# An attention and FFN kernel: scores, values and FFN in blocks, loads issued first, and q and k transposed by DMA instead of TensorE

## The chip, the cores and the metric

The kernel runs on one core of one Trainium2 chip. The metric is the device time of one launch in microseconds (us). Besides timed launches there is one profiled execution of each kernel; its length on the core is called the span, and it is about 1.7 to 1.8 us shorter than the time of the same launch. All launches quoted here count as fast runs: no second, slower state was seen, and the granted TensorE clock, a mean over the span, was between 0.97 and 1.0 in all of them.

Engines are named as in the profile: PE is the matrix engine (TensorE), PEld its weight load, DVE is VectorE, ACT is ScalarE, POOL is GpSimd, SP is SyncE. In this kernel POOL and SP issue the DMAs. "L181" is a line of the kernel that was profiled, so line numbers differ from kernel to kernel.

## The reference, cut to what matters

Block-sparse attention over 4 batches, 8 heads, 768 positions and 64 channels, followed by a multiplicative feed-forward network.

```python
scores = scale * np.matmul(q, k.transpose(0, 1, 3, 2))       # [4, 8, 768, 768], D = 64
mask = near the diagonal | first and last block | 3 random blocks per row of 32-blocks
attn = softmax(np.where(mask, scores, -1e9))
x = np.matmul(attn, v) -> [3072, 512]
a = x @ w1                                                    # 512 x 1024
b = x @ w2
h = a * b @ w3                                                # 1024 x 1024
out = h @ w_out                                               # 1024 x 512, float32
```

The kernel folds `w3 @ w_out` into one matrix once, so that the FFN needs three matrix products per token block (`pa`, `pb`, `po`).

## The kernel before

The work is cut into 72 groups, 18 per batch. A group is (b, t, Q, kp): a batch, a third of the queries, four heads, and two of the six key chunks. For each group PE makes two tiles of scores (two heads each, four matmuls 64x128 on 256 columns); ACT takes the exponential of a tile (1.025 us), and DVE multiplies it by the mask (0.69 us). The values of a group are taken one group later, so that ACT and DVE have time. After every third group the output `o` is divided by the denominator `d`: ACT does a logarithm and an exponential, DVE a multiplication, and only then can the next values write `o` and `d`, which have one buffer each.

Everything else PE has to do is put into a queue of "fill" items, and `pop(n)` emits n of them: first the weight fold (`fold_transpose`, four PE transposes and a DVE copy; `fold_mm`, four matmuls 128x512), later the FFN (`pa`, `pb`, `po`, four matmuls 128x512 each). The order in which PE, ACT and DVE get their instructions is the order of the program.

```python
ps_s = pool("ps_s", 2, space=PSUM)    # score tiles, and also the PE transposes of q and k
ps_o = pool("ps_o", 1, space=PSUM)    # o and d
ps_f = pool("ps_f", 2, space=PSUM)    # all fill items

def transposes(b, pr):                # q and k of two heads: [token, channel] -> [channel, token]
    tp = ps_s.tile([128, 2, 1024], BF16, tag="s", name="tp")
    for x, src in ((0, qn[b, pr]), (1, kn[b, pr])):
        for c in range(C):
            for h in range(2):
                nc.tensor.transpose(tp[64 * h:64 * h + 64, x, c * 128:(c + 1) * 128],
                                    src[:, h, c, :], ident)
    t = qkt.tile([128, 2, S], BF16, tag="qkt", name="qkt")
    nc.vector.tensor_copy(t, tp[:, :, :S])
    QK[b, pr] = t

# (cut: scores, values, normalize, ffn)

for i in range(NF):                   # NF = 8: all fold transposes first ...
    fill.append(fold_transpose(i, 0))
    fill.append(fold_transpose(i, 1))
for i in range(NF):                   # ... then all fold matmuls
    fill.extend(fold_mm(i))

for s, g in enumerate(groups):
    b, t, Q, kp = g
    r = s % 18
    # (cut: transposes(0, 2) and (0, 3) at groups 5 and 7)
    if b + 1 < B:
        if r in (2, 5, 8, 11):
            load_pair(b + 1, (r - 2) // 3)
        if r in (12, 13, 15, 16):
            transposes(b + 1, (12, 13, 15, 16).index(r))
    n = 0 if s < 7 else (3 if s < 18 else 2)
    scores(b, t, Q, kp, 0)
    pop(n // 2)
    scores(b, t, Q, kp, 1)
    if prev is not None:
        values(*prev)
        finish(prev)                  # normalizes after kp == 2, and queues FFN items
    pop(n - n // 2)
    prev = g
```

The softmax here doesn't subtract the row's maximum and nothing guards it: scores larger than these inputs give would overflow.

Of the kernel before, what the change touches and what calls it, by code (L numbers as in the profile page):

```python
# [8 lines left out]

F32 = mybir.dt.float32  # L10
BF16 = mybir.dt.bfloat16
I32 = mybir.dt.int32
AF = mybir.ActivationFunctionType
ALU = mybir.AluOpType
# [4 lines left out]
def kernel(  # L19
# [16 lines left out]
    nc = tc.nc  # L36
    B, H, S, D = q.shape
    BLK = 32
    NB = S // BLK
    C = S // 128  # L40
    d_model = H * D
    d_ff = moe_w1.shape[1]
    NF = d_ff // 128
# [3 lines left out]
    def pool(name, bufs, **kw):  # L47
        return ctx.enter_context(tc.tile_pool(name=name, bufs=bufs, **kw))

    const = pool("const", 1)  # L50
    wts = pool("wts", 1)
    nat = pool("nat", 4)
    natv = pool("natv", 8)
    qkt = pool("qkt", 8)
# [24 lines left out]
    rand_sb = const.tile([NB, 6], I32, tag="rand_sb")  # L79
    nc.sync.dma_start(out=rand_sb, in_=sampled_blocks.bitcast(I32))  # L80

    def load_pair(b, pr):
        for src, dst, pl, tag in ((qv, qn, nat, "qn"), (kv, kn, nat, "kn"), (vv, vn, natv, "vn")):
            t = pl.tile([128, 2, C, D], BF16, tag=tag, name=tag)
            nc.gpsimd.dma_start(out=t, in_=src[b][:, 2 * pr:2 * pr + 2])  # L85
            dst[b, pr] = t

    w1_sb = wts.tile([128, 4, d_ff], BF16, tag="w1")
    w2_sb = wts.tile([128, 4, d_ff], BF16, tag="w2")
    w3_sb = wts.tile([128, NF, d_ff], BF16, tag="w3")  # L90
    w3t_sb = wts.tile([128, NF, d_ff], BF16, tag="w3t")
    wo_sb = wts.tile([128, NF, d_model], BF16, tag="wo")
    wf_sb = wts.tile([128, NF, d_model], BF16, tag="wf")

    def load_w12(ap, t):
        src = ap.rearrange("(Q g s d) f -> g d Q s f", Q=2, g=4, s=2)
        for g in range(4):
            for Q in range(2):
                nc.gpsimd.dma_start(out=t[32 * g:32 * g + 32, 2 * Q:2 * Q + 2, :], in_=src[g][:, Q])


    ident = const.tile([128, 128], BF16, tag="ident")
    make_identity(nc, ident)
    ones = const.tile([128, 32], BF16, tag="ones")
    nc.vector.memset(ones, 1.0)

    hot = const.tile([NB, C, 128], BF16, tag="hot")
    nc.gpsimd.memset(hot, 1.0)
    nc.gpsimd.affine_select(out=hot, in_=hot, compare_op=ALU.is_ge, fill=0.0, base=0,
                            pattern=[[1, C], [C, 128]], channel_multiplier=-BLK)  # L110
    nc.gpsimd.affine_select(out=hot, in_=hot, compare_op=ALU.is_ge, fill=0.0, base=BLK - 1,
                            pattern=[[-1, C], [-C, 128]], channel_multiplier=BLK)
    JJ = const.tile([NB, NB], F32, tag="JJ")
    nc.gpsimd.iota(JJ, pattern=[[1, NB]], base=0, channel_multiplier=0,
                   allow_small_or_imprecise_dtypes=True)
    II = const.tile([NB, NB], F32, tag="II")
    nc.gpsimd.iota(II, pattern=[[0, NB]], base=0, channel_multiplier=1,
                   allow_small_or_imprecise_dtypes=True)
    DD = const.tile([NB, NB], F32, tag="DD")
    nc.gpsimd.iota(DD, pattern=[[-1, NB]], base=0, channel_multiplier=1,  # L120
                   allow_small_or_imprecise_dtypes=True)
    load_pair(0, 0)
    load_pair(0, 1)

    A = const.tile([NB, NB], F32, tag="A")
    nc.vector.tensor_tensor(DD, DD, DD, op=ALU.mult)
    nc.vector.tensor_scalar(A, in0=DD, scalar1=1.0, scalar2=None, op0=ALU.is_le)
    for src in (II, JJ):
# [5 lines left out]
    for r in range(3):  # L134
# [3 lines left out]
                                op=ALU.is_equal)  # L138
# [21 lines left out]
    QK = {}  # L160

    def transposes(b, pr):
# [5 lines that stand above are left out]
                                        src[:, h, c, :], ident)  # L168
        t = qkt.tile([128, 2, S], BF16, tag="qkt", name="qkt")
        nc.vector.tensor_copy(t, tp[:, :, :S])  # L170
        QK[b, pr] = t

    E = {}

    def scores(b, t, Q, kp, i):
        qk = QK[b, 2 * Q + i]
        s = ps_s.tile([128, 2, 512], F32, tag="s", name="s")
        for k2 in range(2):
            kc = 2 * kp + k2
            for h in range(2):  # L180
                nc.tensor.matmul(s[:, h, k2 * QT:(k2 + 1) * QT],  # L181
                                 lhsT=qk[64 * h:64 * h + 64, 1, kc * 128:(kc + 1) * 128],
                                 rhs=qk[64 * h:64 * h + 64, 0, t * QT:(t + 1) * QT],
                                 start=True, stop=True)
        e = epool.tile([128, 2, 512], BF16, tag="e", name="e")
        nc.scalar.activation(e, s, AF.Exp, scale=1.0 / 8.0)  # L186
        nc.vector.tensor_tensor(e, e, mask[:, t, kp:kp + 1, :].to_broadcast((128, 2, 512)),  # L187
                                op=ALU.mult)
        E[b, t, Q, kp, i] = e
# [43 lines left out]
    fill = deque()  # L233

    def fold_transpose(i, jh):
        def go():
            tp = ps_f.tile([128, 4, 128], BF16, tag="f", name="w3p")
            for j in range(4):
                nc.tensor.transpose(tp[:, j, :],  # L239
                                    w3_sb[:, i, (4 * jh + j) * 128:(4 * jh + j + 1) * 128], ident)  # L240
            nc.vector.tensor_copy(w3t_sb[:, 4 * jh:4 * jh + 4, i * 128:(i + 1) * 128], tp)  # L241
        return go

    def fold_mm(i):
        box = {}

        def part(jh):
            def go():
                if jh == 0:
                    box["p"] = ps_f.tile([128, 512], F32, tag="f", name="wp")  # L250
                for j in range(4 * jh, 4 * jh + 4):
                    nc.tensor.matmul(box["p"], lhsT=w3t_sb[:, j, i * 128:(i + 1) * 128],  # L252
                                     rhs=wo_sb[:, j, :], start=j == 0, stop=j == NF - 1)
                if jh == 1:
                    nc.vector.tensor_copy(wf_sb[:, i, :], box["p"])
            return go
        return [part(0), part(1)]
# [48 lines left out]


    transposes(0, 0)
    transposes(0, 1)
    load_pair(0, 2)  # L310
    load_pair(0, 3)
    nc.gpsimd.dma_start(out=w3_sb, in_=moe_w3.rearrange("(c r) f -> r c f", r=128))
    nc.gpsimd.dma_start(out=wo_sb, in_=moe_w_out.rearrange("(c r) f -> r c f", r=128))
    load_w12(moe_w1, w1_sb)
    load_w12(moe_w2, w2_sb)
    for t in range(NT):
        build_mask(t)

# [6 lines left out]
    for i in range(NF):  # L325
        fill.append(fold_transpose(i, 0))
        fill.append(fold_transpose(i, 1))
    for i in range(NF):
        fill.extend(fold_mm(i))

    done = {}
# [3 lines left out]
    def finish(g):  # L335
        nonlocal n_ffn
        b, t, Q, kp = g
        if kp == 2:
            normalize(b, t, Q)
            done[b * NT + t] = done.get(b * NT + t, 0) + 1  # L340
            while done.get(2 * n_ffn) == 2 and done.get(2 * n_ffn + 1) == 2:
                ffn(n_ffn)
                n_ffn += 1

    def pop(n):
        for _ in range(n):
            if fill:
                fill.popleft()()

    for s, g in enumerate(groups):  # L350
        b, t, Q, kp = g
        r = s % 18
        if b == 0 and s == 5:
            transposes(0, 2)
        if b == 0 and s == 7:
            transposes(0, 3)
        if b + 1 < B:
            if r in (2, 5, 8, 11):
                load_pair(b + 1, (r - 2) // 3)
            if r in (12, 13, 15, 16):  # L360
                transposes(b + 1, (12, 13, 15, 16).index(r))
        n = 0 if s < 7 else (3 if s < 18 else 2)
        scores(b, t, Q, kp, 0)
        pop(n // 2)
        scores(b, t, Q, kp, 1)
        if prev is not None:
            values(*prev)
            finish(prev)
        pop(n - n // 2)
        prev = g  # L370
    values(*prev)
    finish(prev)
# [33 lines left out]
```

## Time and profile before

| quantity | value | where it is read |
|---|---|---|
| time, median of 3 launches | 308.6 us (307.41 to 308.62) | launch times |
| profiled span | 305.1 us | page |
| PE busy | 93% | busy table |
| chain that ended last | 85% PE | chain of waits |
| start of group 0 (first scores) | 19.17 us | timeline |
| start of group 18 (batch 1) | 80.28 us | timeline |
| start of group 71 (the last) | 264.50 us | timeline |
| a steady group | 3.36 us | timeline, group to group |

From the page of the kernel before: the busy table (busy us, share of the span, instructions), the chain that ended last by engine, the group of DVE copies that empty the transposes (operation, shapes, count, then busy us and mean ns of one, then idle time before them and what ended it), and the DMA queue that loads inputs (packets, MB, share of 16 engines).

```profile
PE 282.8 (93%) x3412; PEld 129.2 (42%) x3412; DVE 188.1 (62%) x303; ACT 194.1 (64%) x250; POOL 48.0 (16%) x78
...
q0 software_dynamic: 16416, 14.68, 31.2%
...
PE 85%; ACT 6%; DVE 3%; POOL 2%; DMA 2%; issue 1%; ACTq 0%; POOLq 0%
...
L170 DVE COPY qkt<-tp 128x1536 bf16<-128x1536 bf16 x16 | 15.3, 956 | 7.0 <-PE tp L167 6.5
```

PE bounds the kernel. Where its time goes is better read from start to start in the timeline of PE than from durations: the length of a matmul record includes a tail in which the next matmul already runs (below, the record of 140.82 lasts 1.04 us, and the next one starts 0.97 us after it). The columns of the timeline are start in us, length in us, engine and line, operation, tiles, shapes and count, and in brackets the idle time before it and what ended that. First the start of the kernel before, then one of its steady groups, between 140.50 and 143.85 us.

```profile
7.37 0.60 PE L147 MATMUL gp<-hot,Ab 24*24 24x512 bf16 x1 [7.37 <-DVE Ab L141]
...
19.17 1.03 PE L181 MATMUL s<-qkt 64*128 64x256 bf16 x8
...
59.98 1.90 PE L252 MATMUL wp<-wo_sb,w3t_sb 128*128 128x512 bf16 x8
61.82 0.39 PE L181 MATMUL s<-qkt 64*128 64x256 bf16 x4
...
66.03 0.53 PE L167 MATMUL tp<-ident,qn 128*64 128x128 bf16 x12
66.39 0.50 PE L167 MATMUL tp<-ident,kn 128*64 128x128 bf16 x12
66.83 0.39 PE L181 MATMUL s<-qkt 64*128 64x256 bf16 x4
...
140.82 1.04 PE L281 MATMUL pb<-x,w_sb 128*128 128x512 bf16 x4
141.79 0.39 PE L181 MATMUL s<-qkt 64*128 64x256 bf16 x4
142.12 0.40 PE L211 MATMUL o<-e,vn 128*32 128x256 bf16 x8
...
142.88 1.04 PE L270 MATMUL pa<-x,w_sb 128*128 128x512 bf16 x4
143.85 0.39 PE L181 MATMUL s<-qkt 64*128 64x256 bf16 x4
```

Three things are to be seen. The mask chain on DVE delivers its result at 7.37 us and scores begin at 19.17 us. A block of 24 transposes takes PE from 66.03 to 66.83, which is 0.80 us, and it stands ahead of scores. In a steady group PE alternates between tile shapes: an FFN item (128x128) lasts 0.97 us from start to start, a tile of scores (64x128) 0.33, the values (128x32) 0.76. The shape changes five times in a group: scores, FFN, scores, values, FFN, and scores again. Where eight matmuls of an FFN item's shape follow each other without a change, as the fold's do from 59.98 to 61.82, they take 1.84 us, not twice 0.97.

### The profile page before, as it was taken

The page shows a single profiled execution, that of the slowest core. Times are in us where ns is not written, and L with a number is a line of the kernel's source. Part 1 is how long each engine was busy: PE and PEld are TensorE (multiplying, and loading weights), DVE is VectorE, ACT ScalarE, POOL GpSimd, SP SyncE. Part 2 cuts the span into 40 slices and gives each one's busy share as a digit, 9 for nine tenths or more (in the row PEclk, how much of TensorE's full clock was granted, in tenths as well). Part 3 has the DMA queues.
Part 4 walks back from the last instruction along what each step waited for, and adds up shares of the span by engine and source line. Part 5 has one row for each costly group of instructions (what it writes and reads, how often), then busy time and mean ns, then how long its engine had stood idle before and what let it go on. Part 6 is the DMA issues. An engine that isn't in the chain of part 4 may idle for free.

```text
span 305.1 us, 7802 instructions
## 1 busy us (share of the span) xinstructions
PE 282.8 (93%) x3412; PEld 129.2 (42%) x3412; DVE 188.1 (62%) x303; ACT 194.1 (64%) x250; POOL 48.0 (16%) x78
## 2 busy tenths in 40 slices
PE   0677787999999999999999999999999999999994
PEld 0434455444444434454444344444344444444441
DVE  4326788767656766776676567676656765643332
ACT  1198875544778866777777787568777777831310
POOL 9940387411100000231100000000000000000000
PEclk9999999999999999999999999999999999999999
DMA  3999999927030012747411000011000110003003
GB/s 50 171 209 210 208 188 200 201 44 102 0 54 2 0 50 91 104 56 103 56 71 69 2 2 2 37 69 37 2 2 1 71 72 0 2 2 138 0 3 134
DMA packets 19941, 21.46 MB, mean 70 GB/s; under 512 B 1476, under 2 KB 14788, under 8 KB 19908
## 3 DMA queue, kind: packets, MB, share of 16 engines
q0 software_dynamic: 16416, 14.68, 31.2%
q1 hardware_dynamic: 3492, 6.29, 5.5%
q8 instruction: 26, 0.43, 0.6%
q14 instruction: 7, 0.06, 0.1%
HBM read 29.36 MB, written 6.29 MB: 117 GB/s over the span
## 4 chain that ended last, share of the span: by engine, by line
PE 85%; ACT 6%; DVE 3%; POOL 2%; DMA 2%; issue 1%; ACTq 0%; POOLq 0%
PE pb L281 15%; PE po L291 15%; PE pa L270 15%; PE s L181 14%; PE o L211 12%; PE wp L252 5%; PE d L208 5%; ACT e L186 4%; PE tp L167 3%; DMA kn<-in_k_dram 2%; DVE e L187 1%; ACT mask L157 1%; PE mp L155 1%; PE w3p L239 1%; DVE w3t_sb L241 1%
## 5 line engine op out<-in xcount | busy, mean ns | idle before, releaser
L186 ACT ACTIVATE e<-s 128x1024 bf16<-128x1024 f32 x144 | 146.7, 1025 | 47.5 <-PE s L181 42.1
L187 DVE TENSOR_TENSOR e<-e,mask 128x1024 bf16<-128x1024 bf16 x144 | 99.4, 690 | 79.2 <-ACT e L186 79.0
L181 PE MATMUL s<-qkt 64*128 64x256 bf16 x576 | 57.3, 280 | 3.7 <-ACT e L186 2.3
L211 PE MATMUL o<-e,vn 128*32 128x256 bf16 x1152 | 54.0, 277 | 1.3 <-DVE x L227 1.1
L273 ACT CAST a<-pa 128x512 bf16<-128x512 f32 x48 | 28.1, 586 | 37.2 <-PE pa L270 37.2
L281 PE MATMUL pb<-x,w_sb 128*128 128x512 bf16 x192 | 49.6, 381 | 0.4 <-DVE h L283 0.4
L270 PE MATMUL pa<-x,w_sb 128*128 128x512 bf16 x192 | 49.7, 381 | 0.0
L291 PE MATMUL po<-wf_sb,h 128*128 128x512 bf16 x192 | 47.3, 381 | 0.0
L208 PE MATMUL d<-e,ones 128*32 128x256 bf16 x576 | 41.8, 275 | 0.0
L181 PEld LDWEIGHTS <-qkt 64*128 64x128 bf16 x576 | 17.6, 95 | 54.4 <-issue 51.5
L283 DVE TENSOR_TENSOR h<-pb,a 128x512 bf16<-128x512 f32 x48 | 32.9, 685 | 10.7 <-PE pb L281 10.7
L211 PEld LDWEIGHTS <-vn 128*32 128x32 bf16 x1152 | 25.2, 96 | 18.0 <-issue 17.2
L281 PEld LDWEIGHTS <-w_sb 128*128 128x128 bf16 x192 | 15.5, 97 | 23.4 <-issue 11.0
L291 PEld LDWEIGHTS <-h 128*128 128x128 bf16 x192 | 16.1, 97 | 21.9 <-issue 6.8
L270 PEld LDWEIGHTS <-w_sb 128*128 128x128 bf16 x192 | 15.7, 98 | 21.7 <-issue 8.0
L296 DVE COPY ob<-po 128x512 f32<-128x512 f32 x24 | 16.5, 687 | 8.1 <-PE po L291 8.1
L85 POOL DMA_DIRECT2D qn<-in_q_dram x16 | 11.6, 725 | 61.9 <-PE tp L167 60.8
L170 DVE COPY qkt<-tp 128x1536 bf16<-128x1536 bf16 x16 | 15.3, 956 | 7.0 <-PE tp L167 6.5
L227 DVE TENSOR_TENSOR x<-o,rec 128x512 bf16<-128x512 f32 x24 | 16.6, 692 | 2.2 <-ACT rec L226 1.8
L208 PEld LDWEIGHTS <-ones 128*32 128x32 bf16 x576 | 16.4, 98 | 0.3
L252 PE MATMUL wp<-wo_sb,w3t_sb 128*128 128x512 bf16 x64 | 15.7, 381 | 0.0
L85 POOL DMA_DIRECT2D vn<-in_v_dram x16 | 11.5, 717 | 19.9 <-PE d L208 18.7
(53 smaller groups left out, 122.2 us busy)
## 6 DMA issues: line engine op xcount, KB each, us to landing
out_dram<-ob SPq DMA_DIRECT2D x24, 256.0 KB, 2.0
qn<-in_q_dram POOLq DMA_DIRECT2D x16, 192.0 KB, 5.4
kn<-in_k_dram POOLq DMA_DIRECT2D x16, 192.0 KB, 5.7
vn<-in_v_dram POOLq DMA_DIRECT2D x16, 192.0 KB, 6.1
w_sb<-in_moe_w_dram POOLq DMA_DIRECT2D x1, 2048.0 KB, 16.9
w_sb<-in_moe_w_dram POOLq DMA_DIRECT2D x16, 128.0 KB, 5.9
wo_sb<-in_moe_w_out_dram POOLq DMA_DIRECT2D x1, 1024.0 KB, 21.6
rand_sb<-in_sampled_blocks_dram SPq DMA_DIRECT2D x1, 0.6 KB
```

Of the source, the lines that this page charges most:

```text
L85: nc.gpsimd.dma_start(out=t, in_=src[b][:, 2 * pr:2 * pr + 2])
L181: nc.tensor.matmul(s[:, h, k2 * QT:(k2 + 1) * QT], lhsT=qk[64 * h:64 * h + 64, 1, kc * 128:(kc + 1) * 128], rhs=qk[64 * h:64 * h + 64, 0, ...
L186: nc.scalar.activation(e, s, AF.Exp, scale=1.0 / 8.0)
L187: nc.vector.tensor_tensor(e, e, mask[:, t, kp:kp + 1, :].to_broadcast((128, 2, 512)), op=ALU.mult)
L208: nc.tensor.matmul(d[rows, :], lhsT=ones, rhs=rhs, start=first, stop=last, skip_group_check=True)
L211: nc.tensor.matmul(o[rows, part * QT:(part + 1) * QT], lhsT=vn[b, 2 * Q + i][:, h, kc, 32 * part:32 * part + 32], rhs=rhs, start=first and ...
L252: nc.tensor.matmul(box["p"], lhsT=w3t_sb[:, j, i * 128:(i + 1) * 128], rhs=wo_sb[:, j, :], start=j == 0, stop=j == NF - 1)
L270: nc.tensor.matmul(p, lhsT=w1_sb[:, c, f * 128:(f + 1) * 128], rhs=x[:, c, :], start=c == 0, stop=c == 3)
L273: nc.scalar.copy(a, p)
L281: nc.tensor.matmul(p, lhsT=w2_sb[:, c, f * 128:(f + 1) * 128], rhs=x[:, c, :], start=c == 0, stop=c == 3)
L283: nc.vector.tensor_tensor(hT[:, f, :], p, box["a"], op=ALU.mult)
L291: nc.tensor.matmul(box["o"], lhsT=hT[:, f, n * 128:(n + 1) * 128], rhs=wf_sb[:, f, :], start=f == 0, stop=f == NF - 1)
```

## The change

It does three things, with one intent: give PE less to do and fewer shape changes.

1. **Crossbar.** For batches 1 to 3, q and k are loaded with channels of two heads side by side (in pieces of 128 B) and transposed by 24 transposing DMAs from one part of SBUF to another, issued by SP ("the crossbar" is the name here for these DMAs). That takes 288 of 384 transposes from PE and 12 copies of 0.96 us from DVE.
2. **Blocks.** Within a group the two tiles of scores stand together, then the values, then two fill items together. The weight fold is interleaved (two transposes, two matmuls per row block) and begins at group 3, not group 7, at two items a group, not three.
3. **Early loads.** POOL issues nearly all loads before anything else; constants come from two new iotas and DVE comparisons in place of POOL selects; w3 is loaded in eight parts.

```diff
+    load_pair(0, 0, "qk")
+    # (cut: iotas, and between them load_pair(0, 1, "qk"))
+    load_pair(0, 0, "v")
+    load_pair(0, 1, "v")
+    nc.gpsimd.dma_start(out=wo_sb, in_=wo_v)
+    load_w3(0, 2)
+    load_pair(0, 2)
+    load_w3(2, 4)
+    load_pair(0, 3)
+    load_w3(4, NF)
+    load_w12(moe_w1, w1_sb)
+    load_w12(moe_w2, w2_sb)
+    # (cut: ident, ones, hot by comparisons on DVE; only now the mask chain)
...
+    def load_pair_t(b, pr):
+        load_pair(b, pr, "v")
+        t = qkt.tile([128, 2, S], BF16, tag="qkt", name="qkt")
+        for x, src in enumerate((qd, kd)):
+            n = nat.tile([128, C, 2, D], BF16, tag="nt", name="nt")
+            for h in range(2):
+                nc.gpsimd.dma_start(out=n[:, :, h, :], in_=src[b][:, :, 2 * pr + h, :])
+            nc.sync.dma_start_transpose(out=t[:, x, :].rearrange("r (c p) -> r c p", c=C),
+                                        in_=n.rearrange("p c h d -> p (c h d)"))
+        QK[b, pr] = t
...
         fill.append(fold_transpose(i, 1))
-    for i in range(NF):
         fill.extend(fold_mm(i))
...
-        n = 0 if s < 7 else (3 if s < 18 else 2)
         scores(b, t, Q, kp, 0)
-        pop(n // 2)
         scores(b, t, Q, kp, 1)
         if prev is not None:
             values(*prev)
             finish(prev)
-        pop(n - n // 2)
+        if b + 1 < B and r in (2, 5, 8, 11):
+            load_pair_t(b + 1, (r - 2) // 3)
+        if b == 0 and s in (7, 8):
+            transposes(0, s - 5)
+        pop(0 if s < 3 else 2)
         prev = g
```

More of the change, by code (lines that the diff above doesn't have):

```diff
@@ L7 @@
 from concourse._compat import with_exitstack
-from concourse.masks import make_identity
 F32 = mybir.dt.float32
@@ L80, with load_pair @@
     nc.sync.dma_start(out=rand_sb, in_=sampled_blocks.bitcast(I32))
-    def load_pair(b, pr):
+    def load_pair(b, pr, which="qkv"):
         for src, dst, pl, tag in ((qv, qn, nat, "qn"), (kv, kn, nat, "kn"), (vv, vn, natv, "vn")):
-            t = pl.tile([128, 2, C, D], BF16, tag=tag, name=tag)
-            nc.gpsimd.dma_start(out=t, in_=src[b][:, 2 * pr:2 * pr + 2])
-            dst[b, pr] = t
+            if tag[0] in which:
+                t = pl.tile([128, 2, C, D], BF16, tag=tag, name=tag)
+                nc.gpsimd.dma_start(out=t, in_=src[b][:, 2 * pr:2 * pr + 2])
+                dst[b, pr] = t
     w1_sb = wts.tile([128, 4, d_ff], BF16, tag="w1")
@@ L99, in load_w12 @@
                 nc.gpsimd.dma_start(out=t[32 * g:32 * g + 32, 2 * Q:2 * Q + 2, :], in_=src[g][:, Q])
-    ident = const.tile([128, 128], BF16, tag="ident")
-    make_identity(nc, ident)
-    ones = const.tile([128, 32], BF16, tag="ones")
-    nc.vector.memset(ones, 1.0)
-    hot = const.tile([NB, C, 128], BF16, tag="hot")
-    nc.gpsimd.memset(hot, 1.0)
-    nc.gpsimd.affine_select(out=hot, in_=hot, compare_op=ALU.is_ge, fill=0.0, base=0,
-                            pattern=[[1, C], [C, 128]], channel_multiplier=-BLK)
-    nc.gpsimd.affine_select(out=hot, in_=hot, compare_op=ALU.is_ge, fill=0.0, base=BLK - 1,
-                            pattern=[[-1, C], [-C, 128]], channel_multiplier=BLK)
+    load_pair(0, 0, "qk")
+    idf = const.tile([128, 128], F32, tag="idf")
+    nc.gpsimd.iota(idf, pattern=[[-1, 128]], base=0, channel_multiplier=1,
+                   allow_small_or_imprecise_dtypes=True)
+    load_pair(0, 1, "qk")
+    hotf = const.tile([NB, C, 128], F32, tag="hotf")
+    nc.gpsimd.iota(hotf, pattern=[[1, C], [C, 128]], base=0, channel_multiplier=-BLK,
+                   allow_small_or_imprecise_dtypes=True)
     JJ = const.tile([NB, NB], F32, tag="JJ")
@@ L118, with load_w3 @@
                    allow_small_or_imprecise_dtypes=True)
+    load_pair(0, 0, "v")
+    load_pair(0, 1, "v")
+    wo_v = moe_w_out.rearrange("(c r) f -> r c f", r=128)
+    nc.gpsimd.dma_start(out=wo_sb, in_=wo_v)
+    def load_w3(lo, hi):
+        for i in range(lo, hi):
+            nc.gpsimd.dma_start(out=w3_sb[:, i, :], in_=moe_w3[128 * i:128 * i + 128, :])
+    load_w3(0, 2)
[5 more added lines that the diff above has]
+    load_w12(moe_w2, w2_sb)
+    ident = const.tile([128, 128], BF16, tag="ident")
+    nc.vector.tensor_scalar(ident, in0=idf, scalar1=0.0, scalar2=None, op0=ALU.is_equal)
+    ones = const.tile([128, 32], BF16, tag="ones")
+    nc.vector.memset(ones, 1.0)
+    hot = const.tile([NB, C, 128], BF16, tag="hot")
+    hot_hi = const.tile([NB, C, 128], BF16, tag="hot_hi")
+    nc.vector.tensor_scalar(hot, in0=hotf, scalar1=0.0, scalar2=None, op0=ALU.is_ge)
+    nc.vector.tensor_scalar(hot_hi, in0=hotf, scalar1=float(BLK), scalar2=None, op0=ALU.is_lt)
+    nc.vector.tensor_tensor(hot, hot, hot_hi, op=ALU.mult)
     DD = const.tile([NB, NB], F32, tag="DD")
-    nc.gpsimd.iota(DD, pattern=[[-1, NB]], base=0, channel_multiplier=1,
-                   allow_small_or_imprecise_dtypes=True)
-    load_pair(0, 0)
-    load_pair(0, 1)
+    nc.vector.tensor_sub(DD, II, JJ)
     A = const.tile([NB, NB], F32, tag="A")
@@ L170, in transposes @@
         nc.vector.tensor_copy(t, tp[:, :, :S])
+        QK[b, pr] = t
+    qd, kd = (x.rearrange("b h (p c) d -> b p c h d", c=C) for x in (q, k))
+    def load_pair_t(b, pr):
[7 more added lines that the diff above has]
+                                        in_=n.rearrange("p c h d -> p (c h d)"))
         QK[b, pr] = t
@@ L309 @@
     transposes(0, 1)
-    load_pair(0, 2)
-    load_pair(0, 3)
-    nc.gpsimd.dma_start(out=w3_sb, in_=moe_w3.rearrange("(c r) f -> r c f", r=128))
-    nc.gpsimd.dma_start(out=wo_sb, in_=moe_w_out.rearrange("(c r) f -> r c f", r=128))
-    load_w12(moe_w1, w1_sb)
-    load_w12(moe_w2, w2_sb)
     for t in range(NT):
@@ L352 @@
         r = s % 18
-        if b == 0 and s == 5:
-            transposes(0, 2)
-        if b == 0 and s == 7:
-            transposes(0, 3)
-        if b + 1 < B:
-            if r in (2, 5, 8, 11):
-                load_pair(b + 1, (r - 2) // 3)
-            if r in (12, 13, 15, 16):
-                transposes(b + 1, (12, 13, 15, 16).index(r))
-        n = 0 if s < 7 else (3 if s < 18 else 2)
         scores(b, t, Q, kp, 0)
-        pop(n // 2)
         scores(b, t, Q, kp, 1)
```

## The prediction

> **What bounds it now.** PE. The page's busy table has PE at 93%, the chain of waits is 85% PE, ACT is 64%, DVE 62%. By the timeline: the first scores issue at 19.17 us, behind mask building; batch 0 (18 groups, ACT-bound gaps, weight fold) runs to 80.4; then 54 groups of 3.36 us with PE never idle, plus eight q/k transpose blocks of 0.80 us, to 268; then a drain to 305.1 us.
>
> **Steady group, before** (timeline, matmul starts): scores 0.33 + FFN item 0.97 + scores 0.33 + values 0.76 + FFN item 0.97 = 3.36 us. Eight FFN matmuls issued together take 1.84 us, not 1.94, so each change of tile shape costs about 0.11 us.
>
> **Steady group, after.** The two score tiles stand together (estimate 0.54), then values 0.76, then eight FFN matmuls 1.84: 3.14 us. Two shape changes go, saving 0.22 us. But a new wait appears. Both exponentials (1.025 us each) now sit ahead of the logarithm, reciprocal and DVE normalization: the last ends about 3.92 us after the first scores issue, while the next values, which reuse the single output and denominator buffers, would start at 3.68. I expect PE to wait 0.3 us once per three groups.
>
> **Costs, step by step.**
> - Groups 18 to 71: 54 x 3.14 + 18 x 0.3 = 175 us, against 187.6 including eight transpose blocks (6.4 us): -12.6 us.
> - Batch 0: fold items start at group 3, not 7, and are interleaved; four of the six transpose blocks go (3.2 us). Estimate 53 to 55 us against 61.2: -6 to -8.
> - Drain: 138 items are popped in the loop instead of 141, so three FFN items move there: +2.8 us.
> - Start: q and k land earlier (the second k landed at 12.8 us), but the mask chain on DVE gets its iotas only after four load issues (0.72 us each on POOL) and must first do three 24x768 operations. Its result came at 7.3 us; I estimate 10 to 11.5. First scores at about 20.7 us: +1.5.
>
> **DMA.** Each later pair needs 3072 descriptors of 128 B. The packet records show 79 ns for 768 B and 22 ns for 4 B; interpolated, about 32 ns, or 6 us per pair on 16 engines. [...] Batch 1 loads after the weights (about 41 us) and is needed near 74 to 85 us: some slack.
>
> Sum: about 288.5 us of profile span against 305.1, or 292 us timed. Allowing for unforeseen waiting: **294.5 us**, range 287 to 302. Chances: faster by over 2% 0.87, within 2% 0.09, slower 0.04.
>
> **What would show it.** PE transposes 24 x 4 = 96 instead of 384; a steady group of 3.1 to 3.3 us in the timeline; in the waits, PE "o" on DVE "x" of 4 to 8 us in total, 0.2 to 0.5 us each; group 18 at 72 to 77 us; first scores at 19.5 to 22 us.
>
> **What would make it wrong.** Transposing DMAs or 128 B descriptors several times slower than estimated, so that scores of batch 1 wait for them, or output stores queue behind them on SP until DVE and PE stall; back-to-back scores leaving PE waiting on the two score buffers; a larger normalization wait (0.6 us or more would eat the shape-change gain).

The sum has the transposing DMAs at no cost, and its four steps (-12.6, -6 to -8, +2.8, +1.5) on 305.1 us give 288.8 to 290.8 us of span, where it is put at about 288.5.

## The result, and the profile after

| kernel | median us | lowest to highest | launches | span us |
|---|---|---|---|---|
| before | 308.0 | 306.47 to 308.62 | 4 | 305.1 |
| after | 288.88 | 288.58 to 289.45 | 4 | 286.8 |

The ratio is 0.9388, with a 95% interval of 0.9346 to 0.9431. A ratio here is the mean time of one kernel's fast runs over the mean of the other's of the same rounds, so it is not quite the ratio of the medians. The output was correct.

The span divides at the starts of groups, read from the timelines (the first score matmul of groups 0, 18 and 71). The four differences add up to the whole, -18.3 us.

| stretch | before | after | difference |
|---|---|---|---|
| start, to group 0 | 19.17 | 19.88 | +0.7 |
| batch 0, group 0 to 18 | 61.11 | 53.86 | -7.25 |
| group 18 to 71 | 184.22 | 170.64 | -13.6 |
| group 71 to the end | 40.60 | 42.42 | +1.8 |

The page of the kernel after, the same parts as above, with one more queue:

```profile
PE 260.8 (91%) x3124; PEld 132.3 (46%) x3124; DVE 183.8 (64%) x296; ACT 188.8 (66%) x250; POOL 71.5 (25%) x105
...
q0 software_dynamic: 47632, 14.69, 50.9%
q1 hardware_dynamic: 22692, 11.02, 18.5%
...
PE 62%; DMA 12%; ACT 12%; DVE 5%; POOL 5%; issue 3%; POOLq 0%; ACTq 0%
```

PE has 288 instructions fewer, as many as transposes were taken away, and its busy time fell by 22 us. Its busy share barely moved, from 93% to 91%, while the kernel became 6% faster. The share hides the gain, since busy time and span fell together, and a record of 1.04 us stands for a step of 0.97 us. The chain says more: PE's part in it fell from 85% to 62%, because ACT (6% before, 12% after), DVE (3% and 5%) and loads (DMA, 2% and 12%) now take turns in it.

The timeline of PE after, first its start, then one steady group (93.53 to 96.68 us) and the beginning of the next:

```profile
10.58 0.60 PE L167 MATMUL gp<-hot,Ab 24*24 24x512 bf16 x1 [10.58 <-DVE Ab L161]
...
19.88 1.03 PE L214 MATMUL s<-qkt 64*128 64x256 bf16 x8
...
93.53 0.61 PE L214 MATMUL s<-qkt 64*128 64x256 bf16 x8
94.07 0.40 PE L244 MATMUL o<-e,vn 128*32 128x256 bf16 x8
...
94.84 1.04 PE L303 MATMUL pa<-x,w_sb 128*128 128x512 bf16 x4
95.72 1.03 PE L314 MATMUL pb<-x,w_sb 128*128 128x512 bf16 x4
96.68 0.61 PE L214 MATMUL s<-qkt 64*128 64x256 bf16 x8
97.41 0.40 PE L244 MATMUL o<-e,vn 128*32 128x256 bf16 x8
```

The two score tiles together take 0.54 us from start to start (before: twice 0.33), the values 0.77, two FFN items together 1.84 (before: twice 0.97): 3.15 us by these starts, and 3.14 or 3.15 in the others without a normalization. There are three shape changes in place of five, and each one that went saved about 0.11 us.

In the next group the values start 0.73 us after the scores, not 0.54. That is the predicted new wait, 0.19 us long. The chain of waits of the kernel after, in order of time (start, length, what), shows who is in it:

```profile
94.89 1.02 ACT e L219
95.90 0.29 ACT ln L257
...
96.21 0.43 ACT rec L259
...
96.66 0.70 DVE x L260
...
97.41 0.40 PE o L244 x8
```

The second exponential stands ahead of the logarithm and the reciprocal on ACT; then DVE normalizes, which frees `o`. It comes once per three groups: 90.39 to 93.53, 93.53 to 96.68, 96.68 to 100.01 are groups of 3.14, 3.15 and 3.33 us. Yet the view of waits (total us, times, longest us) lists nothing of it; the two waits that its second line here counts are in batch 0 (0.63 us before 30.57 and 1.05 before 69.27):

```profile
POOL nt L201 <- DMA qkt<-nt: 38.3, 7, 21.2
...
PE o L244 <- DVE x L260: 1.7, 2, 1.1
```

The record of the scores from 96.68 lasts to 97.29, so only 0.12 us of idle time is left before 97.41 in the records, and the timeline line of 97.41 carries no bracket: the views leave out so short a gap. A short wait behind matmuls whose records overlap like this is to be read from start to start. The other line, POOL waiting 38.3 us for a transposing DMA to release a load buffer, is harmless: no instruction of PE waits for `qkt` from a DMA in this kernel. The two transposes of the last pair of batch 1 were issued at 67.6 and 69.2 us, and the last of their packets ended at 74.7; PE first reads that pair at about 84.2.

The view of DMA issues (tiles, queue, operation, count, median us from issue to landing) has the crossbar:

```profile
qkt<-nt SPq DMA_TRANSPOSE x24, 5.8
```

Loads from HBM landed after a median of 5.6 us (`nt`, 96 KB) and 5.8 us (`vn`, 192 KB). The packets of 256 B that the transposing DMAs use had a median of 18 ns each, the 128 B packets of the loads 32 ns. No plain DMA with the same packets between parts of SBUF ran beside them, so how a transposing DMA compares with one is not shown. Issuing one holds SP for a median of 1.22 us. All 24 stand on one queue, and the outputs were correct.

### The profile page after: what moved, and what is told of

The parts are those of the page before. It is cut to its first block, busy times and chain, and to the rows that moved or that the text cites. A ratio compares the mean times of both kernels' runs of the same rounds, so it can differ in the third digit from the quotient of the medians.

```text
span 286.8 us, 7359 instructions
## 1 busy us (share of the span) xinstructions
PE 260.8 (91%) x3124; PEld 132.3 (46%) x3124; DVE 183.8 (64%) x296; ACT 188.8 (66%) x250; POOL 71.5 (25%) x105
## 4 chain that ended last, share of the span: by engine, by line
PE 62%; DMA 12%; ACT 12%; DVE 5%; POOL 5%; issue 3%; POOLq 0%; ACTq 0%
PE pa L303 13%; PE o L244 12%; PE pb L314 12%; DMA w_sb<-in_moe_w_dram 11%; PE po L324 10%; ACT e L219 7%; PE s L214 7%; DVE x L260 4%; PE d L241 4%; PE wp L285 3%; ACT rec L259 3%; ACT ln L257 2%; DMA nt<-in_q_dram 2%; POOL w_sb L99 1%; POOL vn L85 1%
## 5 line engine op out<-in xcount | busy, mean ns | idle before, releaser
L219 ACT ACTIVATE e<-s 128x1024 bf16<-128x1024 f32 x144 | 139.1, 1021 | 47.7 <-PE s L214 47.6
L214 PE MATMUL s<-qkt 64*128 64x256 bf16 x576 | 46.8, 277 | 3.5 <-ACT e L219 3.5
L324 PE MATMUL po<-wf_sb,h 128*128 128x512 bf16 x192 | 44.5, 380 | 0.0
L214 PEld LDWEIGHTS <-qkt 64*128 64x128 bf16 x576 | 22.8, 95 | 34.7 <-issue 32.0
L244 PEld LDWEIGHTS <-vn 128*32 128x32 bf16 x1152 | 27.5, 96 | 22.0 <-issue 19.2
L314 PEld LDWEIGHTS <-w_sb 128*128 128x128 bf16 x192 | 18.7, 98 | 24.1 <-issue 2.6
L201 POOL DMA_DIRECT2D nt<-in_q_dram x24 | 19.7, 824 | 40.2 <-DMA qkt<-nt 35.9
L324 PEld LDWEIGHTS <-h 128*128 128x128 bf16 x192 | 17.5, 98 | 22.3 <-issue 3.4
L303 PEld LDWEIGHTS <-w_sb 128*128 128x128 bf16 x192 | 15.7, 98 | 21.7 <-issue 8.0
L201 POOL DMA_DIRECT2D nt<-in_k_dram x24 | 19.6, 821 | 4.3 <-DMA qkt<-nt 2.3
L177 ACT CAST mask<-mp 128x512 bf16<-128x512 f32 x9 | 4.8, 587 | 13.7 <-PE mp L175 13.7
```

Source lines behind the costliest of these rows:

```text
L201: nc.gpsimd.dma_start(out=n[:, :, h, :], in_=src[b][:, :, 2 * pr + h, :])
L214: nc.tensor.matmul(s[:, h, k2 * QT:(k2 + 1) * QT], lhsT=qk[64 * h:64 * h + 64, 1, kc * 128:(kc + 1) * 128], rhs=qk[64 * h:64 * h + 64, 0, ...
L219: nc.scalar.activation(e, s, AF.Exp, scale=1.0 / 8.0)
L244: nc.tensor.matmul(o[rows, part * QT:(part + 1) * QT], lhsT=vn[b, 2 * Q + i][:, h, kc, 32 * part:32 * part + 32], rhs=rhs, start=first and ...
L303: nc.tensor.matmul(p, lhsT=w1_sb[:, c, f * 128:(f + 1) * 128], rhs=x[:, c, :], start=c == 0, stop=c == 3)
L314: nc.tensor.matmul(p, lhsT=w2_sb[:, c, f * 128:(f + 1) * 128], rhs=x[:, c, :], start=c == 0, stop=c == 3)
```

## The experiments

Twelve kernels were run, in three sessions on different chips, each beside the kernel before. The medians of the kernel before were 306.88, 306.83 and 307.11 us in them. "Ratio" is against the kernel before of the same session; the kernel after has 0.9388. All outputs were correct.

My theory was the prediction's sum: PE bounds the kernel, so each part is worth the PE time that it takes away, plus or minus the waits named. The rival was that parts act through something else: through the buffers in PSUM that the transposes and the fold share with other work, or through DMA. The first session therefore undoes or does one part at a time.

### After, with PE transposes (the crossbar undone)

```diff
-            load_pair_t(b + 1, (r - 2) // 3)
+            load_pair(b + 1, (r - 2) // 3)
+        if b + 1 < B and r in (12, 13, 15, 16):
+            transposes(b + 1, (12, 13, 15, 16).index(r))
```

> The kernel after with the crossbar undone: q and k of batches 1 to 3 are loaded as before and transposed by PE, after the values of the same groups. My theory (each of the 12 transpose blocks is 0.80 us on the PE chain and the crossbar is hidden): 288.9 + 9.6 = 298.5 us, 297 to 301 as a block also takes one of the two score buffers. Rival (the gain lies in the early loads and the order, and the crossbar only moves work between engines that have room): 289 to 291 us.

Measured: 300.38 us (299.57 to 300.65), ratio 0.9775 [0.9756, 0.9795], in the range. Per batch, four blocks of transposes cost 3.5 us in batch 0 (57.38 against 53.86 from group 0 to 18), 4.0 in batch 1 and 4.0 in batch 2 (61.70 against 57.75 from group 36 to 54), and nothing in batch 3, which has none. That is 0.95 us a block, where PE's own part is 0.80. The rest is waiting. The view of waits lists scores that wait for DVE's copy of the transposes:

```profile
PE s L214 <- DVE qkt L190: 3.9, 7, 1.5
```

A block of transposes takes one of the two score buffers and holds it until DVE has copied it out. Of the 3.9 us, 3.0 lie in three waits of batch 0, and in exchange 1.9 us of waits for the exponential went (1.6 us in this view, 3.5 in that of after). In batches 1 and 2 two blocks of four are followed by such a wait of 0.21 us; the other two begin 0.20 us late themselves, which the view doesn't list. That they too wait for a score buffer is likely, but not shown.

### Before, with the crossbar alone

`load_pair_t` in place of `load_pair` and `transposes` in the loop of before, nothing else.

> The kernel before with the crossbar alone. My theory: eight blocks of 0.80 us go in the PE-bound stage and four in batch 0, where ACT bounds some of the time: 308 - 6.4 to - 9.6 = 298.5 to 301.5 us. Rival: 306 to 309 us.

Measured: 299.54 us (299.13 to 299.95), ratio 0.9757 [0.9741, 0.9772], in the range. From group 18 to 36 it takes 60.42 us against 63.57, from 36 to 54 60.41 against 63.59: 3.2 us, four blocks of 0.80 and no more. In the order of before, a fill item stands between the two score tiles, and the copy has time: in before a group with a block takes 4.15 us, which is 3.36 and 0.79. In batch 0 the gain was only 0.8 us: its first seven groups took 2.4 us longer than before's, with PE waiting for the exponential.

### Before, with the blocks alone

```diff
         scores(b, t, Q, kp, 0)
-        pop(n // 2)
         scores(b, t, Q, kp, 1)
         if prev is not None:
             values(*prev)
             finish(prev)
-        pop(n - n // 2)
+        pop(n)
```

> The kernel before with the order alone: both score tiles, values, then all fill items of the group. My theory: 54 groups go from 3.36 to 3.21 us (-8.1 us), batch 0 gains about 2 us from the 11 groups with fill: 298 to 301 us. Rival (order matters little as PE is busy either way, or the normalization wait eats it): 305 to 309 us.

Measured: 314.53 us (313.88 to 315.43), ratio 1.0247 [1.0222, 1.0272]. The expectation was wrong, in sign. The steady groups did become shorter: from group 54 to 71, where nothing is transposed, it takes 55.40 us against 57.06, which is 3.26 a group. But batch 0 took 69.47 us against 61.11, and batches 1 and 2 about 1.0 us each more than before. The waits view, then two lines of its timeline:

```profile
PE s L181 <- DVE qkt L170: 9.5, 13, 0.7
...
PE w3p L239 <- DVE w3t_sb L241: 6.9, 5, 2.3
```

```profile
48.90 0.58 PE L239 MATMUL w3p<-ident,w_sb 128*128 128x128 bf16 x4 [2.27 <-DVE w3t_sb L241]
...
129.69 0.40 PE L181 MATMUL s<-qkt 64*128 64x256 bf16 x4 [0.73 <-DVE qkt L170]
```

Two causes are plain in it. The second tile of scores, with no fill item ahead of it any more, waits 0.73 us for the copy of the transposes to give its score buffer back. And three fold transposes in a row need three of the two fill buffers, so that the third waits up to 2.27 us for a DVE copy. A third one is smaller: in two stretches of 3.4 us, from 48.6 and from 58.8 us on, the granted clock was 0.50. In the first of them the group is no longer than its neighbour (4.02 us against 4.72), since PE waits there anyway; the second can have cost at most 1.7 us, half its length. The order alone costs 7.65 us in all. Neither expectation was met; of the two theories at the head of this section, the one of buffers holds here beside that of PE time.

### Before, with the early loads alone

The prologue and the order of loads of after in the kernel before.

> The kernel before with the new start alone: loads issued first, iotas and DVE comparisons in place of affine selects, weights in the new order, fold schedule and order as before. My theory: first scores 0.7 us later (19.9 against 19.2 us), nothing else waits for loads: 307.5 to 310 us. Rival (early loads are where the gain of batch 0 comes from): 300 to 304 us.

Measured: 307.9 us (307.38 to 308.58), ratio 1.003 [1.0008, 1.0053], in the range. First scores at 19.74 us (before 19.17), and from there to group 18 61.11 us, the same as before to the digit.

The three parts alone are worth -7.3 us, +7.65 and +1.0: together +1.3. The whole change is worth -19.1. (The blocks of this list leave the fold as it was, so the whole has one part more; the next experiment undoes it. The new fold alone in the old order, and the old order of scores and fill in the kernel after, were not run.)

### After, with the fold of before

```diff
         fill.append(fold_transpose(i, 1))
+    for i in range(NF):
         fill.extend(fold_mm(i))
...
-        pop(0 if s < 3 else 2)
+        pop(0 if s < 7 else (3 if s < 18 else 2))
```

> The kernel after with the fold as before: all 16 transposing items first, then the 16 matmul items, none up to group 6, three per group in groups 7 to 17. Formed after the order alone had made the kernel before slower (314.5 against 306.9 us): with score tiles together the third of three adjacent transposing items waits for a DVE copy to free one of two PSUM buffers (up to 2.3 us a group), and 33 items, an odd number, make the later groups issue pb of one slice ahead of pa of the next. My theory: about 7 us of such waits and 2 to 3 us in the steady groups: 296 to 300 us. Rival (the loss was all due to transposes in the score buffers, which the crossbar has removed here): 288 to 291 us.

Measured: 295.42 us (295.14 to 296.59), ratio 0.9634 [0.9611, 0.9658], slightly under the range. It is 6.5 us slower than after. Batch 0 takes 61.68 us, no less than the 61.11 of before. PE's fold transposes wait 5.9 us in five waits for their DVE copies:

```profile
PE w3p L272 <- DVE w3t_sb L274: 5.9, 5, 2.3
```

The granted clock was 0.50 from 51.8 to 58.6 us in this launch, but the groups there took 4.00 and 4.14 us, less than the three before them (5.13, 4.66 and 4.52), so the clock doesn't explain the loss. From group 18 to 71 it takes 1.7 us more than after. Undoing the fold thus costs 7.8 us in batch 0, more than the whole gain there of 7.25; since undoing the crossbar costs 3.5 us there as well, the parts cannot be added up.

### After, with the loads of before

The prologue and the place of loads of before, everything else as in after.

> The kernel after with the start and load order of before (affine selects, w3 in one load behind all q, k and v of batch 0, first scores at 19.2 us). My theory: w3 lands near 30 us, where the first transposing item of group 3 stands at 28 us, so early loads are worth 1 to 3 us in the new order though nothing in the old one, less 0.7 us of start: 289 to 292 us. Rival (loads are never waited for): 288 us.

Measured: 293.92 us (293.38 to 294.31), ratio 0.9577 [0.9558, 0.9596]. The direction was right; the loss, 5.0 us, is larger than expected. Its timeline:

```profile
30.15 0.62 PE L253 MATMUL w3p<-ident,w_sb 128*128 128x128 bf16 x8 [1.46 <-DMA w_sb<-in_moe_w_dram]
...
35.28 3.53 PE L266 MATMUL wp<-wo_sb,w3t_sb 128*128 128x512 bf16 x8 [3.20 <-DMA wo_sb<-in_moe_w_out_dram]
...
42.65 1.90 PE L266 MATMUL wp<-wo_sb,w3t_sb 128*128 128x512 bf16 x8
```

The fold now begins near 28 us and its weights are not there: PE waits 1.46 and 3.20 us for them. After the wait of 3.20 us, the same eight matmuls take 3.53 us, where the next eight take 1.90: the view of stretches has a granted clock of 0.50 from 35.2 to 38.6 us, and these matmuls start every 0.43 us, the next eight every 0.22. That the wait brought the lower clock is not shown. The 1.6 us so lost is what the expectation had left out. Batch 0 takes 59.57 us against 53.86, and from group 18 on nothing changes. Early loads are thus worth nothing in the old order (+1.0 us) and 5 us in the new one, since only there does PE want the weights early.

### After, with one more item in group 4

The steady groups of after have the pair `pa`, `pb` behind the values. One extra item shifts this to `pb`, `pa`, and so changes what ACT has to do before the normalization. It was meant as a test that the normalization wait is as sensitive as the chain says.

```diff
-        pop(0 if s < 3 else 2)
+        pop(0 if s < 3 else (3 if s == 4 else 2))
```

> The kernel after with three items in group 4 instead of two, so that every later group has pb of one slice ahead of pa of the next. My theory: the copy of pa then ends the group and delays the next exponentials, the wait before the first values of every third group grows from 0.19 to 0.35 us, and steady groups go from 3.21 to 3.26 us mean: 291 to 292 us. Rival (the pairing doesn't matter): within 0.3% of 288.9 us.

Measured: 288.05 us (287.89 to 288.66, five launches), ratio 0.9396 [0.9378, 0.9415], no different from after. The expectation of 291 to 292 us was missed. The profile shows that two effects cancel. The wait did grow, from 0.19 to 0.35 us (0.89 from scores to values, less 0.54), though in only about half of the steady groups that have it; in the others it stayed at 0.19:

```profile
85.19 0.61 PE L214 MATMUL s<-qkt 64*128 64x256 bf16 x8
86.08 0.40 PE L244 MATMUL o<-e,vn 128*32 128x256 bf16 x8 [0.28 <-DVE x L260]
```

From group 18 to 71 it takes 171.53 us against 170.64, 0.9 more. But batch 0 takes 52.69 us against 53.86, 1.2 less. In after, a group with two fold transposes is followed by one with two fold matmuls; shifted, most groups have one of each. That I had not foreseen.

### After, with the fill before the values

If the fill items stand ahead of the values, PE has work while the normalization runs, and the wait of 0.19 us must go.

```diff
+        pop(0 if s < 3 else 2)
         if prev is not None:
             values(*prev)
             finish(prev)
-        pop(0 if s < 3 else 2)
```

> The kernel after with the two fill items between the scores and the values instead of behind the values: same number of shape changes, but over 1 us more between one normalization and the next values. My theory (values wait for the normalization, 0.19 us once per three groups, about 1 us at the group starts of batch 0 that follow transposing items): steady groups 3.14 us each, 283 to 286 us in all. Rival (the 0.19 us is a change of tile shape or the score buffers, not the normalization): 288 to 290 us.

Measured: 289.83 us (288.95 to 290.21), ratio 0.9441 [0.9419, 0.9463]. The expectation of 283 to 286 us was missed. Again the mechanism is there and another one pays for it. Two fold lines of batch 0, and score tiles of three groups that follow each other, over a normalization:

```profile
47.42 3.49 PE L285 MATMUL wp<-wo_sb,w3t_sb 128*128 128x512 bf16 x8
...
55.14 1.90 PE L285 MATMUL wp<-wo_sb,w3t_sb 128*128 128x512 bf16 x8 [0.67 <-DVE w3t_sb L274]
...
88.80 0.61 PE L214 MATMUL s<-qkt 64*128 64x256 bf16 x8
...
91.94 0.61 PE L214 MATMUL s<-qkt 64*128 64x256 bf16 x8
...
95.08 0.61 PE L214 MATMUL s<-qkt 64*128 64x256 bf16 x8
```

All steady groups are now 3.14 us; from group 19 to 71 it takes 163.52 us against 166.76, which is 3.2 us less, or 0.18 us for each of 18 normalizations. But from group 0 to 19 it takes 62.00 us against 57.74. Fold matmuls wait for the DVE copy of the fold transposes, 4.7 us in seven waits: in this order less of PE's other work stands between the two.

```profile
PE wp L285 <- DVE w3t_sb L274: 4.7, 7, 0.7
```

That is not all of it. The group that begins at 43.6 us takes 8.05 us, in after 5.64, and the fold line of 47.42 is in it: eight matmuls in 3.49 us instead of 1.90, at a granted clock of 0.50 (47.6 to 51.0 us). No gap of PE between group 0 and this line was longer than 1.3 us, where the late loads had one of 3.20 just before; what lowers the clock is not shown. This 1.6 us may belong to the profiled launch (290.21 us, mean clock 0.991) more than to the order: the fastest launch, 288.95 us, had a mean clock of 1.0.

### After, with every crossbar transpose issued twice

If the crossbar costs nothing because it is far off the critical path, doubling it costs nothing either.

```diff
-            nc.sync.dma_start_transpose(out=..., in_=...)
+            for _ in range(2):
+                nc.sync.dma_start_transpose(out=..., in_=...)
```

> The kernel after with every crossbar transpose issued twice into the same tile: the result stays right, the crossbar's work doubles to 48 transposes. My theory (the crossbar is off the critical path; in the profile after the last transposes of batch 1 are issued near 70 us, land within 7.2 us, and are first read near 84 us): 288.5 to 291 us. Rival (the crossbar costs time somewhere, hidden in the sum): at least 24 x 1.2 us of SP issue more, and scores waiting for transposes: over 295 us.

Measured: 294.77 us (292.03 to 295.73), ratio 0.9601 [0.9564, 0.9639]. That lies between the two expectations. The profiled launch was the fastest, 292.03 us; its timeline has two waits that after doesn't have:

```profile
86.69 0.39 PE L215 MATMUL s<-qkt 64*128 64x256 bf16 x4 [1.30 <-DMA qkt<-nt]
...
121.71 1.02 PE L315 MATMUL pb<-x,w_sb 128*128 128x512 bf16 x4 [0.88 <-DVE ob L330]
```

The last pair of batch 1 lands 1.30 us too late. And DVE waits 3.0 us in two waits for output stores, which stand behind the transposes on SP, until PE waits 0.88 us for DVE:

```profile
DVE ob L330 <- DMA out_dram<-ob: 3.0, 2, 2.0
```

These two waits of PE, 2.2 us, are most of the 3.4 us that this span is longer than after's; 0.6 us more lie before group 0, in the scatter of the start. The other three launches were 2 to 4 us slower still, and have no profile; why they were is open. Their mean clocks (0.977, 0.998 and 0.994, against 1.0) don't settle it, since the one at 0.998 was 2.1 us slower too. What follows is a bound: the crossbar's work is off the critical path as it is, but twice as much is not. Its margin in batch 1 is some 9 us (74.7 to 84.2), not unlimited.

### After, with the mask chain first

The start of after is later, although its loads are earlier, because the mask chain on DVE waits for its iotas behind four loads on POOL (issues of 0.71 to 0.84 us; the iotas end at 5.54 us) and for work on `hot` (three operations, to 7.1 us).

```diff
+    # (JJ and II iotas moved here)
     load_pair(0, 0, "qk")
...
     nc.vector.tensor_copy(Ab, A)
+    # (ident, ones, hot, hot_hi moved here, behind the mask chain)
```

> The kernel after with the iotas of block indices ahead of the first loads and the one-hot comparisons behind the block-mask comparisons on DVE. My theory (in the new start the block mask comes late, at 10.5 us, and PE stands behind it): first scores at 17 us instead of 19.9, 286 to 287 us in all. Rival (the start is bound by the loads of q and k, or the weights pace batch 0): 288 to 290 us.

Measured: 286.04 us (285.7 to 286.24), ratio 0.9306 [0.9281, 0.933], as expected. The first mask matmul starts at 7.11 us and the first scores at 17.01:

```profile
17.01 1.03 PE L215 MATMUL s<-qkt 64*128 64x256 bf16 x8
```

After group 0 it is the same as after (53.85 us against 53.86 to group 18). Which of the two moves gained how much was not tried.

### After, with a hybrid order, and everything together

The last two use what was learnt: in batch 0 the values before the fill and the fold shifted by one item, from group 19 on the fill before the values. The second adds the mask chain first, and lets DVE do every second copy of the mask, which ACT did alone.

```diff
+        fill_first = s >= 19
+        if prev is not None and not fill_first:
             values(*prev)
             finish(prev)
         # (cut: loads and transposes)
-        pop(0 if s < 3 else 2)
+        pop({0: 0, 1: 0, 2: 0, 4: 3, 18: 1}.get(s, 2))
+        if prev is not None and fill_first:
+            values(*prev)
+            finish(prev)
```

> The kernel after with the fold shifted by one item in batch 0 (so that a transposing item and a matmul item share most groups, as in the shifted run), one item in group 18 to keep pa and pb together later, and the fill before the values from group 19 on. My theory (the earlier run with fill before values lost in batch 0, by fold matmuls waiting for DVE copies, what it gained in the steady groups): batch 0 shorter by about 2 us, steady groups 3.14 us: 282 to 284.5 us. Rival (a fixed loss elsewhere eats it): 288 us.

Measured: 283.79 us (283.31 to 284.3), ratio 0.9234 [0.9205, 0.9263], as expected. From group 0 to 19 55.06 us against after's 57.74, and from 19 to 71 164.19 against 166.76: both gains hold at once.

> The hybrid with the mask chain first and the mask copies shared between ACT and DVE. Theory: gains add up, 278 to 281 us. Rival: with the start 4 us earlier the weights pace batch 0 and part is lost again, 281 to 284 us.

Measured: 280.46 us (279.82 to 280.57), ratio 0.9121 [0.9096, 0.9146], as expected. It beats both kernels: by 8.8% the kernel before, and by 2.8% the kernel after (0.9121 over 0.9388). From its page and its timeline:

```profile
PE 258.0 (93%) x3124; PEld 130.9 (47%) x3124; DVE 183.9 (66%) x300; ACT 184.0 (66%) x246; POOL 71.6 (26%) x105
```

```profile
16.39 1.04 PE L215 MATMUL s<-qkt 64*128 64x256 bf16 x8
```

First scores come 3.5 us earlier than in after, and PE's share is back at 93%, with a span of 278.1 us. The step from the hybrid is 3.3 us, of which the mask chain first explains 2.8 (288.88 less 286.04); what the shared copies add is within the scatter of the start and not shown.

## Why the prediction was right or wrong

The direction was right and the time of 288.9 us lies in the range of 287 to 302; the middle of the prediction, 294.5 us, was 5.6 us too high. The steps, with the terms of the sum against what the trace shows:

| term | predicted | measured |
|---|---|---|
| start | +1.5 us | +0.7 |
| batch 0 | -6 to -8 | -7.25 |
| groups 18 to 71 | -12.6 | -13.6 (group starts 18 to 71) |
| end | +2.8 | +1.8 (from group 71) |
| whole span | 288.5 us | 286.8 us |
| from span to time | +3.5 | +2.1 (medians), +1.8 in the profiled launch |
| for the unforeseen | +2.5 | nothing needed |

- **The steady group: right.** 3.14 us was predicted and 3.14 measured, from 0.54 for the pair of score tiles and 1.84 for the pair of fill items. PE transposes fell to 96 as predicted.
- **The normalization wait: right in kind, over-sized.** The prediction had 0.3 us in one group of three; it is 0.19. Over 18 normalizations that is 2.0 us of the sum. Putting the fill before the values removed it, and with it 3.2 us from group 19 to 71.
- **The step that failed is how the wait would show.** The prediction expected 4 to 8 us in the view of waits, PE "o" on DVE "x", in pieces of 0.2 to 0.5 us. The view has 1.7 us in two pieces, and both are in batch 0: it lists none of the 18 later waits. The waits of 0.19 us are real, as the timeline and the chain show, but the records' tails leave too short a gap for the view.
- **The start: right in kind, within the range given for first scores.** The mask result came at 10.58 us (predicted 10 to 11.5), the first scores at 19.88 (19.5 to 22 named, 20.7 as the best guess). Kernels with this same prologue had their first scores anywhere from 19.73 to 20.51, those with the prologue of before from 19.17 to 19.73. The means, 20.15 and 19.43, are 0.7 us apart, so the later start is real, though one pair of launches would not show it. The scatter goes with the clock: the four profiled launches with the new prologue that start at 19.73 to 19.88 have a full clock for 3.4 us from about 15.1 to 15.6 us on, while PE builds the mask, and 0.50 for the next 6.8 us; the clock record of the four at 20.50 and 20.51 begins only after 27 us. In all of them, and in before, the first eight score matmuls take 1.03 us, later ones 0.61. That the clock is the cause of the scatter was not tested. That the late mask chain costs is shown by moving it forward, which gained 2.9 us at the start.
- **The DMA step: right where it had numbers.** The packets of 128 B took a median of 32 ns, the number interpolated. Transposing DMAs land after 5.8 us, loads from HBM after 5.6 to 5.8. No scores wait for them.
- **From span to time: mis-sized.** I took 3.5 us from the difference of the median of three launches (308.6) and the span of one other launch (305.1). The profiled launch itself had taken 306.75 us, so the term was 1.65. Launches of the kernel before scatter by 2 us, and the two numbers were not of the same launch.
- **What the sum hides.** It was right because all parts were costed in the new order. It reads, though, as if each part had a value of its own. The experiments show that it doesn't: alone, the order costs 7.65 us and early loads 1.0. The crossbar gains 7.3 us in the old order and 11.5 us in the new one (300.38 less 288.88; 11.9 by the ratios). In batch 0 of the new kernel, undoing the crossbar, the fold or the loads costs 3.5, 7.8 and 5.7 us, together more than twice the gain of 7.25 that the prediction hit with 6 to 8. It priced two of these, the 3.2 us of transposes and the fold, and named no dependence on the early loads there: that the total came out right was in part luck. The prediction named the score buffers only as a risk of the new order; that the crossbar is what keeps this risk away, and that the new order loses batch 0 without the new fold, it did not say.
- **Left open.** Why three of four launches with doubled transposes were 2 to 4 us slower than the profiled one, why the first groups of batch 0 were slower with the crossbar alone, and why the end grew by 1.8 us and not 2.8.

## What to carry to other kernels

A block of PE transposes costs its PE time and also the PSUM buffer it borrows until it has been copied out (here 0.80 us, and 0.15 more of waiting in the new order); before changing an order, ask of each item which buffer it takes, whose copy gives it back, and whether its data will have landed at the new, earlier time. Parts of a change tried one by one can each look worthless or harmful and still be needed together, so cost them, and test them, in the final order as well (undo one) as in the old one (do one). Where records of an engine overlap, as PE's do here (0.61 us for a step of 0.54), read short waits from start to start in the timeline, and compare stretches between the same landmarks: twice here, two effects of opposite sign hid behind an unchanged or barely changed total.

## What the traces measured besides

- A change of tile shape costs about 0.11 us here (two score tiles 0.54 us together against twice 0.33, two FFN items 1.84 against twice 0.97), which with two changes fewer in each of 54 groups is an estimate of some 12 us.
- One transposing DMA of 192 KB from SBUF to SBUF holds SP for a median of 1.22 us and lands 2.7 to 7.2 us after its issue, median 5.8. Output stores on the same queue stand behind it: with the transposes doubled, DVE waited 3.0 us for stores.
- In before, the records of the transposes of q and k on PE have a median of 219 ns (384 records); in after they have 266 to 278, and half of the 96 ran before group 0, where a block of 24 took 1.28 us from start to start. But from 66.03 us in before, 24 of them in a row take 0.80 us from start to start, 33 ns each. The length of such a record must not be multiplied by the count.
- A packet of 128 B from HBM took 32 ns (median of 36,864), against 79 ns for 768 B; packets of 256 B between parts of SBUF took 18 ns, less for more bytes. These last differ from the others in size and in place, so which of the two makes the difference is not shown.
- Short waits of PE can be hidden by the tails of its records: a wait of 0.19 us left 0.12 us of idle time, and the view of waits listed none of 18 such waits, which add up to 3.4 us.
